# Retention and two MLPs in one kernel: the decay rates come in as one row and are spread over the partitions by a product

## The chip, the cores and the metric

One core of one Trainium2 chip runs the whole program. Five engines with instruction streams of their own take part: TensorE (PE, its weight loads shown apart as PEld), VectorE (DVE), ScalarE (ACT), GpSimd (POOL) and SyncE (SP), which here only issues DMAs. ScalarE and GpSimd issue some DMAs too. The metric is the device time of one execution in microseconds, the median of several runs; lower is better.

## The reference, cut to what matters

```python
q, k, v: (2, 8, 768, 64) float32      lam: (8,) float32, one decay rate for each head
rel   = pos[:, None] - pos[None, :]
Dmask = np.where(rel >= 0, lam[:, None, None] ** rel, 0.0)        # powers of the rate
for each block of 64 positions:
    intra = (q_b @ k_b.T * Dmask) @ v_b
    inter = (q_b * lam ** (pos + 1)) @ state
    out   = intra + inter
    state = lam ** block * state + (k_b * lam ** (block - 1 - pos)).T @ v_b
x = out as (1536, 512)
x = relu(x @ w_in) ** 2 @ w_out            # first MLP, 512 -> 2048 -> 512
y = h @ w_out2,  h = leaky_relu(x @ w_in2) # second MLP, slope 0.01
```

The eight rates enter everything in the first part: the masks, the scaling of queries and keys, and the decay of the state.

## The kernel before, in words

The first part, `retention`, works on 12 units: 2 batches times 6 chunks of 128 positions, all 8 heads together. For each unit the kernel loads k, q and v (256 KB each, `load`), transposes k and q on TensorE (`transposes`, the result copied to `kqT` by ScalarE), makes the scores (`scores`), multiplies them with the table of powers on VectorE (`mask`, result `Pm`), updates the state (`state`, with the scaled keys `kd` made by GpSimd in `scale_k`), and adds up the output (`output`), which is split in a high and a low part (`xhi`, `xlo`) for the MLPs. The MLPs follow; there every matrix product is done in three products of such parts, and some blocks by sums and differences of blocks. Their products all stand in one helper, `three` (L622).

The order on SP and PE within `retention` is the order in which the code is written; on the other engines a scheduler sets it, except where the code pins a step.

At the start, before the first keys are there, the program does three things that the change touches:

- It loads the rates. `rate` is a tile of 128 partitions by 8 heads; one DMA from ScalarE's queue (L229) reads the same 32 bytes for each of the partitions.
- It keeps TensorE busy with products whose result nobody reads, the warming products: `warm(8)` multiplies a tile of zeros, `none`, with itself eight times (L244), and `warm_half(3)` does three small transposes of the identity between the real transposes (L248). Each fp32 product of `warm` shows as two passes in the trace.
- It makes the tables on VectorE: `of_row` from `rate` (L260, two copies), `LR` from `of_row` (L263, four scans) and `powers` from `rate` (L254, eight scans). `mask` and `scale_k` read `powers`; `scale_q` and the decay of the state read `LR`.

TensorE's results stand in a ring of eight banks (`bank`), handed out in the order of the code; a bank comes free when its reader is done. A DMA's completion is counted on one of eight semaphores in turn, so that a later DMA that takes the same semaphore waits until the earlier one has landed.

Of the kernel before, what the change touches and what calls it, by code (L numbers as in the profile page):

```python
# [9 lines left out]
F32 = mybir.dt.float32  # L10
# [6 lines left out]
P = 128  # L17
# [3 lines left out]
def tile_retention_then_two_mlps(  # L21
# [12 lines left out]
    nc = tc.nc  # L34
    B, H, S, D = q.shape
# [22 lines left out]
    def bank():  # L58
        return psum.tile([P, 512], F32, tag="ps", name="ps")
# [150 lines left out]
    def retention(ctx_att, att):  # L210
# [14 lines left out]
            nats[i, name] = t  # L225

        ve = nc.vector
        rate = att.tile([P, H], F32, name="rate")
        nc.scalar.dma_start(rate, bass.AP(tensor=lam.tensor, offset=lam.offset, ap=[[0, P], [1, H]]))  # L229
        for i in range(2):  # L230
            load(i, "k")
            load(i, "q")
# [3 lines left out]
        make_identity(nc, ident)  # L236
        none = att.tile([P, C], F32, name="none")
        ve.memset(none, 0.0)

        idle = bank()  # L240

        def warm(n):
            for _ in range(n):
                tc.keep_in_program_order(nc.tensor.matmul(idle[:, 0:P], none, none, start=True, stop=True))  # L244
# [2 lines left out]
            for _ in range(n):  # L247
                tc.keep_in_program_order(nc.tensor.transpose(idle[:, 0:D], ident[0:D], ident[0:D, 0:D]))  # L248

        warm(8)  # L250

        powers = att.tile([P, H, C + 1], F32, name="powers")
        for h in range(H):
# [182 lines left out]
    with ExitStack() as ctx_att:  # L436
        att = ctx_att.enter_context(tc.tile_pool(name="att", bufs=1))
        with tc.manual_schedule(engines={mybir.EngineType.SP, mybir.EngineType.PE}):
            retention(ctx_att, att)
# [569 lines left out]
```

## Time and profile before

| what | value |
|---|---|
| median of 3 runs | 556.07 us (555.64 to 557.9) |
| the profiled execution, whole time | 556.28 us |
| its span in the trace | 554.5 us |
| PE busy | 548.7 us, 99% of the span |
| DVE, ACT, POOL busy | 78%, 54%, 16% |
| DMA | 71.86 MB, mean 130 GB/s |

The span runs from the first instruction to the last. The whole time is longer than it by 1.78 us, which lie around it. The busy shares are means over the span; how the first 50 us differ from the rest is seen only in the views by stretch.

### The profile page before, as it was taken

What the parts mean: (1) busy time and instruction counts of PE and PEld (TensorE: products, weight loads), DVE (VectorE), ACT (ScalarE), POOL (GpSimd) and SP (SyncE); (2) the same over time, 40 slices, a digit from 0 to 9 for tenths busy, and PEclk for the clock granted to TensorE, in tenths of its full rate; (3) what the DMA queues carried; (4) which work ended last, traced back from release to release, by engine and by line L of the source; (5) the groups of instructions that cost most, each with busy time, mean ns of one, the idle gap of its engine ahead of it and who ended that gap; (6) DMA issues with size and microseconds to landing.
All of it is one profiled execution on the core that took longest, in us unless ns stands there. A gap on an engine that the chain in (4) does not pass through costs nothing.

```text
span 554.5 us, 8716 instructions
## 1 busy us (share of the span) xinstructions
PE 548.7 (99%) x3393; PEld 470.9 (85%) x3393; DVE 434.6 (78%) x643; ACT 299.8 (54%) x482; POOL 87.0 (16%) x99
## 2 busy tenths in 40 slices
PE   8999999999999999999999999999999999999997
PEld 8989888888888888888888889888898889888997
DVE  6669999997775895639999986969176954967987
ACT  4454898556773357453376385645364464546520
POOL 5864000000213011220000000000213011310041
PEclk9999999999999999999999999999999999999999
DMA  9997245542459615674423221264518743650544
GB/s 204 218 259 238 77 160 182 190 149 80 83 150 196 179 19 134 165 139 130 155 57 115 82 100 47 76 229 139 88 21 168 192 102 52 76 78 0 165 141 151
DMA packets 68056, 71.86 MB, mean 130 GB/s; under 512 B 39856, under 2 KB 43952, under 8 KB 68016
## 3 DMA queue, kind: packets, MB, share of 16 engines
q1 hardware_dynamic: 52208, 54.14, 31.2%
q0 software_dynamic: 6912, 12.59, 15.9%
q10 hardware_dynamic: 8896, 4.59, 2.9%
q8 instruction: 26, 0.43, 0.3%
q14 instruction: 14, 0.11, 0.1%
HBM read 49.29 MB, written 22.02 MB: 129 GB/s over the span
## 4 chain that ended last, share of the span: by engine, by line
PE 96%; DMA 3%; SPq 1%; ACT 0%; issue 0%; DVE 0%; ACTq 0%
PE ps L622 90%; PE ps L303 2%; PE ps L365 1%; PE ps L363 1%; DMA v<-in_v 1%; DMA q<-in_q 1%; PE ps L334 1%; DMA k<-in_k 1%; PE ps L282 1%; SPq L65 1%; ACT kqT L286 0%; DVE res L850 0%; ACTq L286 0%
## 5 line engine op out<-in xcount | busy, mean ns | idle before, releaser
L812 POOL DMA_DIRECT2D spill<-f x48 | 42.5, 891 | 401.6 <-ACT f L808 401.6
L808 ACT COPY f<-ps 128x512 f32<-128x512 f32 x72 | 41.9, 585 | 70.9 <-PE ps L622 70.8
L622 PE MATMUL ps<-xlo,w1h 128*128 128x512 f32 (+1 forms) x190 | 69.2, 368 | 0.0
L622 PE MATMUL ps<-xhi,w1l 128*128 128x512 f32 (+1 forms) x184 | 68.3, 371 | 0.0
L622 PE MATMUL ps<-xhi,w1h 128*128 128x512 f32 (+1 forms) x184 | 68.3, 371 | 0.0
L762 DVE TENSOR_TENSOR f<-ps,f 128x512 f32<-128x512 f32 x70 | 46.2, 687 | 6.2 <-PE ps L622 5.8
L622 PE MATMUL ps<-xhi,sw 128*128 128x512 f32 (+1 forms) x176 | 49.6, 350 | 0.0
L172 DVE TENSOR_TENSOR w2l<-hb,w2h 128x1024 fp32r<-128x1024 f32 x16 | 19.6, 1223 | 36.3 <-ACT w2h L170 36.3
L622 PE MATMUL ps<-g0h,w2h 128*128 128x512 f32 x112 | 43.6, 389 | 0.0
L622 PE MATMUL ps<-g0h,w2l 128*128 128x512 f32 x112 | 43.6, 389 | 0.0
L154 DVE SCALAR_TENSOR_TENSOR hb<-raw,hb 128x1024 uint16<-128x1024 uint32 x31 | 42.4, 1366 | 0.3
L622 PE MATMUL ps<-g0l,w2h 128*128 128x512 f32 x112 | 42.6, 389 | 0.0
L622 PEld LDWEIGHTS ps<-xlo,w1h 128*128 128x128 f32 x190 | 35.5, 189 | 6.1
L622 PE MATMUL ps<-t,sw 128*128 128x512 f32 x168 | 40.4, 389 | 0.0
L551 DVE TENSOR_TENSOR g0l<-f,g0h 128x512 fp32r<-128x512 f32 x52 | 35.1, 686 | 6.7 <-ACT f L547 5.9
L145 ACT ACTIVATE hb<-raw 128x1024 f32<-128x1024 f32 x31 | 35.3, 1149 | 9.3 <-DMA raw<-in_moe_w_in 2.9
L622 PEld LDWEIGHTS ps<-xhi,w1l 128*128 128x128 f32 x184 | 34.7, 188 | 6.2 <-DVE w1l L132 0.4
L622 PEld LDWEIGHTS ps<-xhi,w1h 128*128 128x128 f32 x184 | 34.7, 188 | 6.2 <-ACT xhi L70 0.2
L622 PE MATMUL ps<-w2h,g0h 128*128 128x512 f32 (+1 forms) x104 | 39.6, 381 | 0.0
L622 PE MATMUL ps<-w2l,g0h 128*128 128x512 f32 (+1 forms) x104 | 39.6, 381 | 0.0
L622 PE MATMUL ps<-w2h,g0l 128*128 128x512 f32 (+1 forms) x104 | 38.6, 381 | 0.0
L151 DVE SCALAR_TENSOR_TENSOR hb<-raw,hb 128x1024 uint32<-128x1024 uint32 x31 | 37.9, 1221 | 0.3
(220 smaller groups left out, 1321.9 us busy)
## 6 DMA issues: line engine op xcount, KB each, us to landing
raw<-in_moe_w_out SPq DMA_DIRECT2D x15, 1024.0 KB, 4.9
raw<-in_moe_w_in SPq DMA_DIRECT2D x14, 1024.0 KB, 6.6
spill<-f POOLq DMA_DIRECT2D x48, 256.0 KB, 4.3
spill<-f SPq DMA_DIRECT2D x24, 256.0 KB, 2.3
k<-in_k SPq DMA_DIRECT2D x12, 256.0 KB, 5.1
q<-in_q SPq DMA_DIRECT2D x12, 256.0 KB, 5.1
f<-spill SPq DMA_DIRECT2D x12, 256.0 KB, 2.8
res<-spill SPq DMA_DIRECT2D x12, 256.0 KB, 4.8
```

What stands on the lines that cost most here:

```text
L65: step = queue.dma_start(dst, src)
L145: step = nc.scalar.activation(hf, w_hi.bitcast(F32), AF.Abs)
L151: yield ve.scalar_tensor_tensor(out=hb, in0=w_hi, scalar=0xC0000000, in1=hb, op0=ALU.bitwise_and, op1=ALU.bitwise_or)
L154: step = ve.scalar_tensor_tensor(out=half, in0=w_lo, scalar=2.0 ** -29, in1=half, op0=ALU.mult, op1=ALU.add)
L172: yield ve.tensor_tensor(out=lo, in0=hf, in1=hi, op=ALU.subtract)
L282: nc.tensor.transpose(ps[half][:, p] if early else two[half][:, n, p], src[r, 2 * p:2 * p + 2, :].rearrange("s h d -> s (h d)"), ident[r, r])
L303: nc.tensor.matmul(raw_scores[i][par][:, p, :], kT[i][r, p, :], qT[i][r, p, :], start=True, stop=True)
L551: nc.vector.tensor_tensor(out=glo, in0=r, in1=ghi, op=ALU.subtract)
L622: nc.tensor.matmul(ps, a, b, start=start and n == 0, stop=stop and n == len(ops) - 1, skip_group_check=again)
L762: ve.tensor_tensor(out=out, in0=ps[h, where], in1=other, op=ALU.add)
L808: nc.scalar.copy(f, src)
L812: nc.gpsimd.dma_start(dst, f, accum_op=ALU.add)
```

## The change

The DMA now brings the eight rates into a tile of one partition, `row`, as 32 bytes once. A second tile of one partition, `ones`, is filled with 128 ones on VectorE. Where eight warming products stood there are now five, then one product of `ones` (128 columns, one row) with `row` (one row, 8 columns), whose result is the eight rates in each of 128 partitions, and then two more warming products. VectorE copies the result from its bank to `rate`. All that reads `rate` is as before.

```diff
-        rate = att.tile([P, H], F32, name="rate")
-        nc.scalar.dma_start(rate, bass.AP(tensor=lam.tensor, offset=lam.offset, ap=[[0, P], [1, H]]))
+        row = att.tile([1, H], F32, name="row")
+        nc.scalar.dma_start(row, bass.AP(tensor=lam.tensor, offset=lam.offset, ap=[[H, 1], [1, H]]))
...
+        ones = att.tile([1, P], F32, name="ones")
+        ve.memset(ones, 1.0)
...
-        warm(8)
+        warm(5)
+        in_all = bank()[:, 0:H]
+        nc.tensor.matmul(in_all, ones, row, start=True, stop=True)
+        warm(2)
+        rate = att.tile([P, H], F32, name="rate")
+        ve.tensor_copy(rate, in_all)
```

TensorE's instructions at the start of the program, before: a semaphore named `DMAHW` counts a DMA, the others an engine. L244 is a warming product, L282 a transpose of keys or queries, L248 a small warming transpose.

```order
L244 MATMUL ps<-none 128x128 [waits DVE_49]
L244 MATMUL ps<-none 128x128 x7
L282 MATMUL ps<-delta,k 128x64 [waits DMAHW1_49,Pool_49]
L282 MATMUL ps<-delta,k 128x64 x7
L248 MATMUL ps<-delta 128x64 x3
L282 MATMUL ps<-delta,q 128x64 [waits DMAHW2_49]
```

And now, at the same place (the lines after the change are 2 to 7 higher):

```order
L246 MATMUL ps<-none 128x128 [waits DVE_49]
L246 MATMUL ps<-none 128x128 x4
L254 MATMUL ps<-row,ones 128x8 [waits DMAHW0_49,DVE_49]
L246 MATMUL ps<-none 128x128 x2
L289 MATMUL ps<-delta,k 128x64 [waits DMAHW1_49,Pool_49]
L289 MATMUL ps<-delta,k 128x64 x7
L250 MATMUL ps<-delta 128x64 x3
L289 MATMUL ps<-delta,q 128x64 [waits DMAHW2_49]
```

One of the eight large products is gone, another has become the small one, and the wait for the rates' DMA now stands in TensorE's stream, ahead of the first transposes.

VectorE's instructions at the start of the program, before: the wait for the rates' DMA is that of the first copy to `of_row`.

```order
L238 MEMSET none 128x128
L260 COPY of_row<-rate 64x4 [waits DMAHW0_49]
L260 COPY of_row<-rate 64x4
L263 SCALAR_TENSOR_TENSOR LR<-of_row,none 128x128 [waits DVE_49]
L263 SCALAR_TENSOR_TENSOR LR<-of_row,none 128x128 x3
L254 SCALAR_TENSOR_TENSOR powers<-rate,delta 128x129 [waits Pool_49]
```

And now:

```order
L238 MEMSET none 128x128
L240 MEMSET ones 1x128
L257 COPY rate<-ps 128x8 [waits PE_49]
L267 COPY of_row<-rate 64x4 [waits DVE_49]
L267 COPY of_row<-rate 64x4
L270 SCALAR_TENSOR_TENSOR LR<-of_row,none 128x128 [waits DVE_49]
L270 SCALAR_TENSOR_TENSOR LR<-of_row,none 128x128 x3
L261 SCALAR_TENSOR_TENSOR powers<-rate,delta 128x129 [waits Pool_49]
```

The filling of `ones` and the copy to `rate` are new, and the chain of the tables waits for TensorE where it waited for the DMA. On ScalarE the DMA of `rate` has become that of `row` at the same place; on GpSimd and SP, and on all engines behind this start, the order is the same as before. One wait is new there: the first product of `scores` also waits for VectorE, since the bank that it takes is the one from which `rate` was copied.

## Rows read from the trace of the kernel before

**Rows 1.** The page: span, and busy time of the engines.

```profile
span 554.5 us, 8716 instructions
PE 548.7 (99%) x3393; PEld 470.9 (85%) x3393; DVE 434.6 (78%) x643; ACT 299.8 (54%) x482; POOL 87.0 (16%) x99
```

**Rows 2.** Waits of PE, whole span: us in total, times, longest us.

```profile
PE ps L244 <- DVE none L238: 1.1, 1, 1.1
PE ps L334 <- DMA v<-in_v: 0.7, 1, 0.7
PE ps L282 <- DMA k<-in_k: 0.3, 1, 0.3
```

**Rows 3.** Chain of waits, 0 to 60 us: start us, us, what.

```profile
2.87 1.41 SPq L65
4.28 0.04 issue
4.32 4.16 DMA k<-in_k
8.48 0.14 issue
8.62 0.46 PE ps L282 x8
...
29.72 5.32 DMA q<-in_q
35.05 0.02 issue
35.07 5.95 DMA v<-in_v
41.02 0.14 issue
41.15 0.69 PE ps L334 x16
```

**Rows 4.** Busy time by stretch: us, five engines (x instructions), clock, DMA share, GB/s.

```profile
0.00:10.00 10.00, 8.60 (x97) 8.00 (x99) 5.58 (x17) 4.42 (x11) 3.33 (x11) 1.00 0.84 189
10.00:20.00 10.00, 9.93 (x204) 9.01 (x202) 7.34 (x14) 4.09 (x10) 9.69 (x12) 1.00 1.02 230
20.00:30.00 10.00, 9.97 (x202) 9.21 (x199) 6.25 (x12) 3.90 (x7) 6.90 (x8) 1.00 1.01 228
30.00:40.00 10.00, 10.00 (x200) 9.35 (x201) 6.65 (x13) 4.98 (x9) 6.99 (x7) 1.00 1.07 250
```

**Rows 5.** Timeline of PE, from the start: start us, us, instructions.

```profile
1.06 3.79 PE L244 MATMUL ps<-none 128*128 128x128 f32 x16 [1.06 <-DVE none L238]
4.77 0.69 PE L282 MATMUL ps<-delta,k 64*128 64x64 f32 x8
...
6.22 0.46 PE L282 MATMUL ps<-delta,k 64*128 64x64 f32 x8
...
6.94 1.16 PE L303 MATMUL ps<-kqT 64*128 64x128 f32 x16
7.94 0.41 PE L282 MATMUL ps<-delta,q 64*128 64x64 f32 x8
8.62 0.46 PE L282 MATMUL ps<-delta,k 64*128 64x64 f32 x8 [0.27 <-DMA k<-in_k]
9.08 1.16 PE L303 MATMUL ps<-kqT 64*128 64x128 f32 x16
10.07 0.41 PE L282 MATMUL ps<-delta,q 64*128 64x64 f32 x8
10.46 0.69 PE L334 MATMUL ps<-v,kd 128*64 128x64 f32 x16
10.94 1.07 PE L365 MATMUL ps<-Pm,v 128*64 128x128 f32 x16
```

**Rows 6.** Timeline of the DMA of the rates, of DVE and of POOL, from the start.

```profile
0.74 0.45 ACTq L229 DMA_DIRECT2D rate<-in_lam  x1
3.96 0.34 DVE L260 COPY of_row<-rate 64x4 f32<-64x4 f32 x2 [2.96 <-DMA rate<-in_lam]
4.33 1.37 DVE L263 TENSOR_TENSOR_SCAN LR<-of_row,none 128x128 f32<-128x128 f32 x4
5.62 2.62 DVE L254 TENSOR_TENSOR_SCAN powers<-rate,delta 128x129 f32<-128x129 f32 x8
8.16 1.26 DVE L308 TENSOR_TENSOR Pm<-ps,powers 128x512 f32<-128x512 f32 x2
8.33 2.07 POOL L321 TENSOR_TENSOR kd<-k,powers 128x512 f32<-128x512 f32 x2 [6.10 <-DVE powers L254]
```

**Rows 7.** DMA view, 0 to 4 us: queues, and issues with KB and us to landing.

```profile
q1 hardware_dynamic: 1523, 0.39, 42.3%
q10 hardware_dynamic: 144, 0.00, 1.8%
...
rate<-in_lam ACTq DMA_DIRECT2D x1, 4.0 KB, 3.2
```

**Rows 8.** The shortest landing of the program, DMA view, 545 to 555 us.

```profile
out<-res SPq DMA_DIRECT2D x1, 128.0 KB, 1.9
```

**Rows 9.** The first load of k, by its tile, 0.7 to 1 us.

```profile
L65 SPq DMA_DIRECT2D k<-in_k x1: 417/417/417, 0.7 to 0.7; - x1
...
DMA to landing us min/median/max: 3.6/3.6/3.6
```

**Rows 10.** Views of L244 and L248: durations (ns min/median/max), first and last start.

```profile
L244 PE MATMUL ps<-none x16: 421/421/579, 1.1 to 4.4; 128*128 128x128 f32 x16
...
L248 PE MATMUL ps<-delta x9: 223/261/311, 5.3 to 6.6; 64*128 64x64 f32 x9
```

**Rows 11.** Chain of waits, 500 us to the end.

```profile
499.96 50.98 PE ps L622 x383
550.94 0.02 issue
550.97 0.42 DVE res L850
```

## The prediction

> **What bounds the kernel now.** I read the page first. TensorE is busy for 548.7 of 554.5 us [rows 1], so only what moves its stream, or one of its few idle stretches, can move the end. The waits of PE list those: 1.1 us at the start, before the zeros for the first warming product are there, 0.3 us for a load of keys, and 0.7 us for a load of values [rows 2]. Third, the chain of waits says where the last two lie: the keys of unit 2 land at 8.48 us and TensorE goes on at 8.62; the values of unit 8 land at 41.02 and it goes on at 41.15 [rows 3]. No later wait stands in the list, and the chain is products of L622 down to the last addition at 550.97 [rows 2, 11]. So the end is set by the moment at which the stream goes on at 41.15, and this moment by a landing.
>
> Fourth, the stretches [rows 4]. From 10 to 40 us the DMA engines are busy the whole time (1.01 to 1.07) at 228 to 250 GB/s. In the same stretches TensorE is busy for 9.93 to 10.00 of 10 us. The first 40 us are therefore two full streams side by side, loads and products, which meet at 8.62 and at 41.15, and both times TensorE was the one that waited. A change of TensorE's first microseconds that does not move the loads meets a wait of 0.27 us at 8.62 and one of 0.71 us at 41.15, and is lost in them.
>
> **The change part by part.**
>
> *The load of the rates.* Before, it was issued at 0.74 us, took 0.45 us to issue and landed after 3.2 us, at 3.94; the first copy to `of_row` starts at 3.96 [rows 6, 7]. Now it is 32 bytes once. No row shows so small a load. Its landing is bounded by 1.9 us, the shortest of the program [rows 8], and by the 3.2 us of the load that it replaces, which has the same queue, source and moment. That gives 2.64 to 3.94 us for `row`. I take the middle, about 3.2: the old landing counts the last of many packets among those of the first keys, and now there is one to wait for. The Trainium skill (DMA: Bandwidth & Descriptors, Anatomy of one DMA) puts a nearly constant 2.0 us on a transfer, mostly its completion, which it fitted for DMAs that GpSimd issues; by that the row would be there at about 2.75 us, and TensorE would not wait for it at all. No run here shows it yet.
>
> *What the loads gain.* The 144 packets of that queue took 1.8% of 16 engines in 4 us [rows 7], 0.07 us of each engine. If all of that stands in front of the keys, every later landing comes 0.07 us earlier; if it fell in time in which the engines had nothing to do (up to 4 us queue q1 uses 42.3% of them), nothing. I take 0.07, with 0 and 0.1 as ends. That the 0.45 us of issuing on ScalarE shrink is worth nothing: its next work that someone waits for is the copy of transposed keys, behind 4.77.
>
> *TensorE's start.* The 16 passes of the eight products span 3.79 us from 1.06, and a single one is drawn 0.42 long, so one starts every (3.79 - 0.42) / 15 = 0.225 us [rows 5, 10]. Five products are ten passes: the small product could start at 1.06 + 2.25 = 3.3 us. With the row there at 3.2 it does not wait. It too is two passes, of 8 columns where the others have 128; each costs between nothing and 0.225 us, and I take 0.1, nearer to a transpose of 64 columns (eight in 0.69 us with their tail) than to the large ones. Then four passes, 0.9 us. The end of the warming comes at 3.3 + 0.2 + 0.9 = 4.4 us (4.2 to 4.65), against 1.06 + 16 x 0.225 = 4.66 before. The first transposes need the keys of unit 0, which land at 0.74 + 3.6 = 4.34 [rows 9], and before they started 0.11 behind the end of the warming (4.77 against 4.66). They start at about 4.5 now: 0.25 us earlier, with 0 and 0.4 as ends. This gain ends at the keys of unit 2, which landed at 8.48; of it only the 0.07 us of the loads stay.
>
> *VectorE's tables.* The product's result can be read some 0.35 us behind the start of its last pass (the tail of a pass in rows 10 is 0.31): 3.3 + 0.1 + 0.35 = 3.75. The new copy costs about what one to `of_row` costs, 0.17 (two in 0.34) [rows 6], so `of_row` starts at 3.9 to 4.0, against 3.96: no change. The filling of `ones` costs nothing, since VectorE stands idle for 2.96 us there.
>
> What hides a delay of the tables, if the row is late: `Pm` of unit 0 is done at 8.16 + 1.26 = 9.42 and first read at 10.94, and the first `kd` is done at about 8.33 + 1.03 = 9.36 and read at 10.46 [rows 5, 6]. So 1.1 us of delay cost TensorE nothing; without that cover it would cost what exceeds them. The new wait of the first scores, for the bank that `rate` is copied from, ends near 4 us, and they start at 6.94.
>
> **The sum.** Nothing from TensorE's start, nothing from the tables, 0.07 us from the loads, which the stream would feel at 41.15 too. The profiled execution took 556.28 us, 0.21 above the median; 556.28 - 0.07 = 556.21, and against the median 556.07 - 0.07 = 556.0.
>
> **The rivals.**
>
> *The row is late and TensorE waits for it.* At the 3.94 us of the old landing the small product starts at about 3.95, the warming ends at 3.95 + 0.2 + 0.9 = 5.05 and the transposes start near 5.15: 0.4 us late, with 0.6 as the end at full-length passes. The tables come 0.6 to 0.7 late, which their cover of 1.1 takes. Of TensorE's 0.4 to 0.6 the idle 0.27 at 8.62 takes a part and the 0.71 at 41.15 the rest, if the loads stay as they are. If the loads are held back by buffers that TensorE frees later, some of it reaches the end: 0 to 0.5 us, 556.3. For it speaks the queue shared with the keys, against it the single packet.
>
> *Slower: TensorE's clock rises later.* The column of the clock shows 1.00, the level of 2.4 GHz, in all of these stretches [rows 4], but the passes tell that the first ones go slower: eight transposes of keys take 0.69 us at 4.77 and 0.46 at 6.22 [rows 5], and a small warming transpose 311 ns at most and 223 at least [rows 10]. I read this as 1.2 GHz up to about 6.1 us, after five microseconds without a break. Now there is a product of 8 columns among them, and perhaps a pause for the row. If the rise comes as late again, at about 11, the work between 6.2 and 11.2, some 4.7 us, takes 1.5 to 2 times as long: 2.3 to 4.7 us more, less the idle 0.27 at 8.62 and the 0.71 at 41.15, so 1.3 to 3.7, in the middle 558.5. It decides, that is costs over 0.5% (2.8 us), only when the slow level lasts for four to five microseconds more with no wait to hide them. The Trainium skill (TensorE: Matmul & The Clock Gate, Part 1) has the rule that speaks here: the slow clock is the default, and only sustained activity lifts it, at a moment that varies from run to run. The passes of this trace agree with the slow start; whether the small product disturbs the rise, no row shows.
>
> *The whole of retention moves.* If loads wait for buffers more than for the DMA engines, a stream that starts 0.25 to 0.4 us earlier frees buffers earlier, the values of unit 8 come earlier too, and the wait at 41.15 shrinks with them: 0.3 to 0.7 us, 555.5. Against it speaks the DMA share of 1.0 from 10 to 40 us.
>
> **How the numbers follow.** No change at the end (the sum): 0.70, with its own range of 555.7 to 556.7. Late row: 0.12. Later clock: 0.08, half of it above 0.5%. Moved retention: 0.10, which stays under 0.7 us. About 0.5% is what a measurement of this kernel can tell from no change; 1.0 us of waits at 8.62 and 41.15 and a first wait of 1.1 us that the change does not touch are all that could be gained, so faster by more than that has 0.02, left for what I don't see. Slower by more: 0.04. Within: 0.94. The range reaches from the moved retention and its 0.5 us of scatter (single runs lie from 555.64 to 557.9) to the nearer half of the late clock: 555.0 to 557.6.
>
> **What would show it.** In the changed kernel's trace: a landing of `row` in under 2.5 us and no wait of the small product for it; the first transposes at about 4.5; `of_row` at 3.9 to 4.0; TensorE's wait for the keys of unit 2 longer, at about 0.5 us in all, and its transposes at 8.5 to 8.6 as before; the wait for the values at 41 still there, at 0.6 to 0.8 us. It would be wrong if transposes of 64 columns still take 0.69 us for eight behind 6.2 (the clock), if the values of unit 8 land more than 0.5 us from 41.02 (the loads), or if a wait appears behind 41.15, where none was.

## The result and the profile after

The changed kernel takes 560.3 us (560.06 to 560.78, 6 runs) where the kernel before took 556.02 in the same comparison (6 runs): a ratio of 1.0077, 95% interval 1.0066 to 1.0088, slower by 4.3 us. The forecast was 556.0 and no change, with a range up to 557.6. The profiled execution took 560.49 us, its span is 558.7.

Of the page, the span and the engines' busy time, answering to [rows 1]:

```profile
span 558.7 us, 8720 instructions
PE 550.4 (99%) x3393; PEld 471.9 (84%) x3393; DVE 434.7 (78%) x645; ACT 300.2 (54%) x482; POOL 86.8 (16%) x99
```

TensorE runs the same number of instructions (3393) and its busy time is up by 1.7 us only; the span has grown by 4.2. Its waits over the whole span, answering to [rows 2]:

```profile
PE ps L341 <- DMA v<-in_v: 1.2, 3, 0.6
PE ps L246 <- DVE none L238: 1.1, 1, 1.1
PE ps L341 <- POOL tmp L348: 0.8, 1, 0.8
PE ps L310 <- ACT kqT L297: 0.7, 1, 0.7
PE ps L289 <- DMA q<-in_q: 0.5, 2, 0.3
```

Two waits of 1.0 us in all behind the start have become seven of 3.2 us. All of them lie in retention: the timeline of TensorE shows the first product of the MLPs at 56.94 us, where it stood at 52.67 in the kernel before, and the chain's last addition comes at 555.16 instead of 550.97 [rows 11]. So all of the 4.2 us are lost before 57 us. First the line of the kernel before, then two of the changed one:

```profile
52.67 0.50 PE L622 MATMUL ps<-xhi,w1h 128*128 128x512 f32 x1
```
```profile
56.94 0.50 PE L629 MATMUL ps<-xhi,w1h 128*128 128x512 f32 x1
```
```profile
555.16 0.42 DVE res L857
```

The start of TensorE's timeline, answering to [rows 5]:

```profile
1.06 2.50 PE L246 MATMUL ps<-none 128*128 128x128 f32 x10 [1.06 <-DVE none L238]
3.49 0.59 PE L254 MATMUL ps<-row,ones 1*128 1x8 f32 x2
4.01 1.22 PE L246 MATMUL ps<-none 128*128 128x128 f32 x4
5.16 0.69 PE L289 MATMUL ps<-delta,k 64*128 64x64 f32 x8
```

The first transposes come at 5.16 us, 0.39 later than before, where I had expected 0.25 earlier. But 4.3 us cannot come from there alone. The busy time by stretch, answering to [rows 4], in the same columns, says where to look:

```profile
0.00:10.00 10.00, 8.67 (x87) 7.95 (x89) 5.99 (x19) 4.27 (x11) 2.97 (x11) 1.00 1.04 179
10.00:20.00 10.00, 9.27 (x187) 8.24 (x185) 6.55 (x12) 4.01 (x11) 9.01 (x10) 1.00 1.15 212
20.00:30.00 10.00, 8.68 (x177) 8.11 (x174) 5.99 (x13) 3.61 (x7) 6.96 (x8) 1.00 0.97 192
30.00:40.00 10.00, 9.75 (x189) 8.86 (x187) 5.64 (x11) 4.03 (x8) 4.90 (x5) 1.00 1.01 207
```

The last two columns say most. The DMA engines are about as busy as before (0.97 to 1.15 between 10 and 40 us, where it was 1.01 to 1.07) and move less: 212 GB/s instead of 230, 192 instead of 228, 207 instead of 250. The same loads, with the same packets of 256 bytes, go slower. The DMA view of 5 to 15 us, queue q1 alone (packets, MB, share of 16 engines), first of the kernel before, then of the changed one:

```profile
q1 hardware_dynamic: 9297, 2.34, 103.8%
```
```profile
q1 hardware_dynamic: 8597, 2.17, 136.0%
```

The share is the time that the packets took, summed, over the time of 16 engines; the records of packets overlap, which is how it can be over 100%. Of the 160 us that 16 engines have in 10 us, a packet took 1.038 x 160 / 9297 = 17.9 ns before and 1.36 x 160 / 8597 = 25.3 ns now. The landings are later for it. Of the chain, two of its longest pieces, answering to [rows 3]:

```profile
24.78 7.96 DMA q<-in_q
...
39.85 8.81 DMA q<-in_q
```

Nothing in the code of these loads was changed, and their order is the same. What differs is where they land. The tiles of a pool lie one behind another, and the pools too; `row` takes the 32 bytes that `rate` had, `ones` 512 bytes more in each partition and `rate` 32 more. In the built program all buffers of k, q and v therefore stand 544 bytes further on: the first of k at 165120 before, a multiple of 256, and at 165664 now, 32 bytes past one. These two addresses are those of the program as it was built; no view of the traces shows them, and neither the diff nor the order of the instructions does. What they are worth is for the experiments to show.

How the slow packets begin is seen in two short stretches of the changed kernel, 2.5 to 3.5 us and 3.7 to 5 us:

```profile
q1 hardware_dynamic: 1120, 0.28, 125.0%
```
```profile
q1 hardware_dynamic: 1117, 0.28, 129.4%
```

The loads to the moved places run at 283 GB/s at first, with packets of 1.25 x 16 / 1120 = 17.9 ns, and then fall to 217 GB/s with packets of 1.294 x 20.8 / 1117 = 24.1 ns. So a packet to such a place does not have a fixed price; it is a stream of them that is held to a lower rate.

### The profile page after: what moved, and what is told of

Its sections match the earlier page's. It is cut to its first block, busy times and chain, and to the rows that moved or that the text cites. A ratio compares the mean times of both kernels' runs of the same rounds, so it can differ in the third digit from the quotient of the medians.

```text
span 558.7 us, 8720 instructions
## 1 busy us (share of the span) xinstructions
PE 550.4 (99%) x3393; PEld 471.9 (84%) x3393; DVE 434.7 (78%) x645; ACT 300.2 (54%) x482; POOL 86.8 (16%) x99
## 4 chain that ended last, share of the span: by engine, by line
PE 93%; DMA 5%; SPq 1%; POOL 1%; issue 0%; DVE 0%
PE ps L629 89%; DMA q<-in_q 3%; DMA v<-in_v 2%; SPq L65 1%; PE ps L372 1%; PE ps L310 1%; PE ps L370 1%; PE ps L341 1%; PE ps L289 0%; POOL qS L303 0%; POOL tmp L348 0%; POOL kd L328 0%; DVE res L857 0%
```

## The experiments

Four theories stood against each other. A: the loads are slow because they land off a multiple of 256 bytes. B: TensorE's late start and a later rise of its clock. C: the single packet for the rates leaves the DMA engines in another phase. D: the engines' own reading and writing at shifted addresses. Each ratio below is against runs of the kernel before on the same chip, with its 95% interval.

**The shift alone, in the kernel before.**

```diff
         ve.memset(none, 0.0)
+        att.tile([P, 136], F32, name="pad")
```

> The kernel before, its eight warming products and its load of the rates untouched, with an unused tile of 544 bytes in each partition behind the zeros, which moves the buffers of k, q and v from multiples of 256 bytes to 32 bytes past one, as the changed kernel does by its two new tiles. Theory A (the landing addresses slow the loads): as slow as the changed kernel, 559.5 to 560.8 us, 256-byte packets at a mean of 24 to 26 ns between 5 and 15 us instead of 18, first transposes still at 4.77 us. Theory B (TensorE's later start and the later rise of its clock cost the time): 556.0 us, packets at 18 ns. Theory C (one packet for the rates leaves the DMA engines in another phase): 556.0 us, packets at 18 ns.

560.6 us, ratio 1.0092 (1.0077 to 1.0107). An unused tile costs as much as the whole change. The DMA view of 5 to 15 us has the slow packets, 1.332 x 160 / 8611 = 24.7 ns, at 219 GB/s:

```profile
q1 hardware_dynamic: 8611, 2.17, 133.2%
```

A holds; B and C cannot explain this run, since its TensorE program and its load of the rates are those of before. (In its profiled execution the clock also fell back for some 3 us, see the last section; the two kernels shifted by 64 and 128 bytes, slow alike, show a granted clock of 1.00 between 5 and 15 us.) The first transposes came at 4.85 and not at 4.77. The tables and the work tiles moved here too, which the runs below take apart in part.

**The changed kernel, realigned.**

```diff
         ve.memset(none, 0.0)
+        att.tile([P, 56], F32, name="pad")
```

> The changed kernel with 224 unused bytes more, so that all buffers behind the tables move by 768 bytes in all and stand on multiples of 256 bytes again; the small product and the load of one packet are untouched. Theory A: 555.7 to 556.8 us, packets at 18 ns, first transposes still late at 5.16 us and absorbed by the waits at 8.6 and 41 us. Theories B and C: 560.0 to 560.6 us, B with packets that follow from the late start, C with packets at 24 to 26 ns.

556.77 us, ratio 1.0014 (1.0005 to 1.0024). The 224 bytes give 3.5 us back. The packets take 1.176 x 160 / 10519 = 17.9 ns again, at 267 GB/s, and TensorE waits for no load any more, though its first transposes stand at 5.17. B and C fall here a second time; what remains of the loss is 0.8 us. That aligned places have no such lower rate shows in the stretch of 2.5 to 12 us, where this kernel moves 278 GB/s on end, with packets of 1.23 x 152 / 10476 = 17.9 ns:

```profile
q1 hardware_dynamic: 10476, 2.64, 123.0%
```

**The shift by 64 and by 128 bytes.** The kernel before with a pad of `[P, 16]` and of `[P, 32]` at the same place.

> The kernel before with 64 unused bytes: buffers of k, q and v at 64 bytes past a multiple of 256. Theory A says slow if the boundary that counts is 256 bytes (559.5 to 560.8 us), and 556.0 us with packets at 18 ns if it is 64 bytes. I expect 64 (chance 0.6). Theories B and C: 556.0 us either way.

> The kernel before with 128 unused bytes: buffers of k, q and v at 128 bytes past a multiple of 256. Theory A with the boundary at 256 bytes: slow like the shifts by 32 and 64 bytes, 559.3 to 560.8 us against 555.6, packets at 24 to 26 ns between 5 and 15 us. Theory A with a boundary at 128: 555.6 us, packets at 18 ns. I expect 256 (chance 0.8).

64 bytes: 559.86 us, 1.0077 (1.0062 to 1.0092), 220 GB/s between 5 and 15 us. I had thought 64 would be enough, and it is not. 128 bytes: 560.48 us, 1.0078 (1.0056 to 1.0099), 218 GB/s. So 32, 64 and 128 bytes past a multiple of 256 cost the same within their intervals. In both kernels too the first loads run at the full rate, 271 and 278 GB/s between 3.7 and 4.9 us with packets of 18 ns, before the slow packets set in. The changed kernel, whose full stream of loads began about a microsecond earlier, was down at 217 GB/s by then; so the fall follows the stream and not a moment of the program.

**The work tiles alone.** A pool with one tile of 32 bytes between the pools of k, q, v and those of the work tiles.

```diff
+        gap = ctx_att.enter_context(tc.tile_pool(name="gap", bufs=1))
+        gap.tile([P, 8], F32, name="pad")
         tr = ctx_att.enter_context(tc.tile_pool(name="tr", bufs=3))
```

> The kernel before with 32 unused bytes between the buffers of k, q and v, which stay where they were, and the tiles that the engines write and read (kqT, qS, kd, Pm), which move to 32 bytes past a multiple of 64. Theory A: 556.0 us, packets at 18 ns, since no load lands in these. If it is the engines' own reading and writing at such addresses that costs (theory D): 558 to 560.5 us with packets at 18 ns. B and C: 556.0 us.

555.86 us, 1.0009 (0.9999 to 1.002), packets at 1.097 x 160 / 9827 = 17.9 ns. D falls for the work tiles: where the engines write and read these costs nothing that can be told from noise. The tables, which also move with the shift of the whole, were not moved alone.

**The control: 768 bytes in the kernel before**, which puts the buffers where the realigned kernel has them (a pad of `[P, 192]`).

> The kernel before with 768 unused bytes, which puts the buffers of k, q and v at the very places that they have in the realigned changed kernel (multiples of 2048). The eight products and the load of 128 packets are untouched. If the realigned kernel's fuller loads (267 GB/s between 5 and 15 us, against 236 before) come from the places: the same here, 260 to 275 GB/s, no wait for values at 41 us, and 555.0 to 555.6 us. If they come from the rates' single packet: 230 to 240 GB/s here, a wait near 41 us, and 555.5 to 555.9 us.

556.15 us, 1.0005 (0.9992 to 1.0017), 248 GB/s. Another multiple of 256 is as good as the old one. The realigned kernel's 267 GB/s does not come from its places; whether it comes from the single packet stays open, since two other kernels with the single packet had 249 and 246 GB/s in that stretch, and the two aligned ones with 128 packets, this and the one above, 248 and 249.

**Some of the loads.** Gaps of 32 and 224 bytes around one pool: first the values alone at 32 bytes past a multiple of 256 (the diff), then, with the gaps ahead of k and of v, keys and queries alone.

```diff
...
+        for name, n in (("k", 6), ("q", 4), ("v", 4)):
+            if name == "v":
+                gap = ctx_att.enter_context(tc.tile_pool(name="gap", bufs=1))
+                gap.tile([P, 8], F32, name="pad")
...
+        rest.tile([P, 56], F32, name="pad")
```

> The kernel before with the buffers of v alone at 32 bytes past a multiple of 256 (12 of the 36 loads), k and q aligned, work tiles aligned. Theory A: only packets of loads of v are slow; a third of the loads at 24 to 26 ns instead of 18 gives about a third of the loss of 4.3 to 5 us, 556.5 to 557.5 us, or less where their delay is hidden. If not the landing address but something that comes with any shift of the whole is the cause: 555.6 us.

> The kernel before with the buffers of k and q at 32 bytes past a multiple of 256 (24 of the 36 loads) and those of v and the work tiles on multiples of 256. With v alone shifted the loss was 0.4 us, not a third of 4.3 to 5. If the loss is a ceiling on the rate of loads that are all shifted (218 GB/s between 5 and 15 us), which mixing lifts: 556.5 to 558.5 us here and a mean between 220 and 235 GB/s in that stretch. If the loss only needs shifted keys and queries, since TensorE waits for these first: 559.5 us or more.

Values alone (12 of 36 loads): 556.08 us, 1.0007 (0.9998 to 1.0017); no loss that can be told, where I had expected a third. Taken alone this run would also fit a cause other than the landing addresses; the second kernel speaks against that. Keys and queries alone (24 of 36): 558.02 us, 1.0041 (1.0026 to 1.0057), 225 GB/s. The loss is not in proportion. The values' loads lie between aligned ones and the stretch of 5 to 15 us still moves 244 GB/s; where all loads are shifted it moves 218 to 220. That is what a ceiling on the rate of shifted loads looks like: a few of them fit under it, a full stream of them does not. The packets agree: with the values alone shifted they took 1.102 x 160 / 9626 = 18.3 ns in the mean, where a third of them at 25 ns would give about 20. I had put down both outcomes of the second kernel beforehand, and it came out on the ceiling's side. The granted clock fell in its profiled execution too (0.53 between 8 and 11 us, 0.997 over the whole), but its slowest run, 559.42 us, has 1.00, so the clock is not what its loss rests on. The loss of the whole shift is about twice that of keys and queries alone; how the rest divides between the values and the tables stays open.

**The change at the old places.** `row` and `ones` in a pool of their own behind all others.

```diff
+        small = ctx_att.enter_context(tc.tile_pool(name="small", bufs=1))
...
-        row = att.tile([1, H], F32, name="row")
+        row = small.tile([1, H], F32, name="row")
...
-        ones = att.tile([1, P], F32, name="ones")
+        ones = small.tile([1, P], F32, name="ones")
```

> The changed kernel whole, with its two new tiles behind all others, so that the buffers of k, q and v stand exactly where they stood before. What is left is the change itself: TensorE's start late by 0.4 us, the tables late by 0.4 us, one packet for the rates. Theory A: 555.6 to 556.4 us against 555.6 to 555.7, ratio 1.000 to 1.0015, packets at 18 ns, no wait of TensorE for a load before 41 us above 0.3. If the places explain only part of the 4.3 us: 557 us or more.

556.42 us, 1.0004 (0.9995 to 1.0013, 11 runs). With its tiles out of the way the change costs nothing that a measurement can tell. The first transposes still start at 5.17, and TensorE's waits have become these:

```profile
PE ps L247 <- DVE none L239: 1.1, 1, 1.1
PE ps L311 <- ACT kqT L294: 0.5, 1, 0.5
```

The two waits for loads are gone, and one of 0.5 us for the copied queries has come, which fits a late start that was taken by what had been waiting.

**A late start alone: nine products** (`warm(9)` for `warm(8)` in the kernel before).

> The kernel before with nine warming products where it has eight, nothing else: the first transposes start at about 5.2 us, as late as in the changed kernel, with the rates' load and the tables as before. If a late start of TensorE is lost in its later waits, as the prediction has it: 555.6 to 555.9 us, ratio within 0.0008 of 1. If it is carried to the end: 0.4 us, ratio 1.0008. Under theory B as it stood (late start and late clock cost the 4 us): 558 us or more.

556.23 us, 1.0005 (0.9994 to 1.0017). The first transposes start at 5.20, as the line below shows, and 0.43 us of lateness do not show at the end beyond noise; whether a part of the 0.4 us is carried, this interval of 1.3 us cannot say.

```profile
5.20 0.69 PE L282 MATMUL ps<-delta,k 64*128 64x64 f32 x8
```

**The small product earlier.** The realigned kernel with `warm(2)` ahead of the product and `warm(3)` behind it.

> The realigned changed kernel with the small product behind two warming products, and three behind it: five large products where the changed kernel has seven. The row landed at 1.92 us there, so the product does not wait. First transposes at 4.3 to 4.5 us instead of 5.17, since the keys land at 4.3. If TensorE's late start is what is left of the loss (0.8 us, 0.14%, of the realigned kernel), this one takes it back: 555.2 to 556.0 us. If the moment of the clock's rise is what is left: 555.6 to 557 us, scattered as the realigned kernel is, with the clock's rise in the trace the later the slower the run.

556.07 us, 1.0001 (0.9991 to 1.0011). The timeline of TensorE:

```profile
2.21 0.59 PE L255 MATMUL ps<-row,ones 1*128 1x8 f32 x2
2.73 1.65 PE L247 MATMUL ps<-none 128*128 128x128 f32 x6
4.31 0.69 PE L290 MATMUL ps<-delta,k 64*128 64x64 f32 x8
```

The product starts at 2.21 without a wait for the DMA, so the row is there before that, and the transposes start at 4.31, 0.86 earlier than in the realigned kernel. The time is 0.7 us below that kernel's, and lies just outside the range that I had set for a start carried on and inside that for the clock. The single runs of the two kernels lie in 555.13 to 556.8 and 555.59 to 556.89, their intervals overlap, and against the kernel before there is no gain. Where the 0.8 us of the realigned kernel come from stays open.

## Why the prediction was wrong

The step that failed is the one on the loads, "What the loads gain", where I wrote that every later landing comes up to 0.07 us earlier, or at the least not at all. It took the loads' own speed as given and looked only at what stands in the queue. Between 5 and 45 us the loads of k took 6.0 us to land in the median instead of 5.2, those of q 5.9 instead of 5.2 and those of v 5.3 instead of 4.5, since a packet of their queue took 0.943 x 640 / 26923 = 22.4 ns in the mean there and not 0.818 x 640 / 28087 = 18.6 (25.3 and 17.9 between 5 and 15 us). The values of unit 8 landed at 38.3 + 5.4 = 43.7 us instead of 41.02; a landing more than 0.5 us from there was the sign that I had named for the loads. The premise of the argument, that the end follows the loads, was right, and it is why the error was so dear: two full streams side by side had 1.0 us of slack between them, and one of the two lost 8 to 17% of its rate between 10 and 40 us.

It was not among my rivals, and slower by more than 0.5% had a chance of 0.04, though what was needed could be read: the change puts two more tiles into the pool `att`, and the code opens that pool ahead of those of k, q and v. The Trainium skill (DMA: Bandwidth & Descriptors, How a descriptor splits into AXI transactions) says that a transaction has to start at a multiple of 256 bytes, so that a descriptor which starts past one needs one transaction more. By that, as an estimate from the page's rule, 256 bytes at 32, 64 or 128 past a multiple take two where they took one, all three alike. The three equal losses agree with it, and so does the shift by 768. But the page gives the rule for what a transaction reads; here it is the side written, in SBUF, that was shifted, and no run here shows the side read. Nor does a count of transactions say by itself why the first loads to the shifted places ran at 283 GB/s with packets of 17.9 ns. That the landing places of keys and queries cost the time is shown; by what mechanism they hold a stream to 218 to 220 GB/s is not.

Point by point, the rest.

- *The row is there in time*: right, but by more than my bounds allowed. In the changed kernel the two packets of its queue stand in the DMA view of 1.6 to 1.7 us, and in the kernel with the earlier product TensorE used the row at 2.21, ahead of the 2.64 to 3.94 that I worked out from rows. From its issue at 0.74 that is 1.5 us at most, less than the 2.0 us by the Trainium skill (DMA: Bandwidth & Descriptors, Anatomy of one DMA), which would have had it at 2.75.
- *The small product costs 0.2 us*: wrong. The ten passes ahead of it are over at 1.06 + 2.50 - 0.42 + 0.21 = 3.35, the last four started at 4.01 only, and they took 1.22 us with their tail, where four of the steady stream take 0.42 + 3 x 0.21 = 1.05. The transposes came at 5.16 where two passes of 0.1 would have let them start at 4.5. The size of this term was 0.2; it measured 4.01 - 3.35 = 0.66, and with the slower four passes behind it about 0.8. The rival of the late row had named 5.15 for the transposes; that it was met is luck, since the row was not late.
- *The tables do not move*: they moved by 0.36 us, with `of_row` at 4.32 and not at 3.96, inside the cover of 1.1 us that I had worked out. VectorE's rows:

```profile
4.12 0.17 DVE L257 COPY rate<-ps 128x8 f32<-128x8 f32 x1 [2.98 <-PE ps L254]
4.32 0.34 DVE L267 COPY of_row<-rate 64x4 f32<-64x4 f32 x2
```

- *What TensorE's start loses or gains is lost in its later waits*: not contradicted, and not shown. The kernel at the old places and the one with nine products have ratios of at most 1.0013 and 1.0017 at the upper end, and 0.4 us carried to the end would be 1.0008.
- *The rival of the later clock*: the fast passes did come later in the profiled execution, though the column of the clock shows 1.00 there as before. Eight transposes of keys at 6.7 us, one of them apart, still took long (the seven in 0.64 us, where eight took 0.46 before), but the kernel at the old places has this too and is not slower, so it is not what made the 4.3 us.
- *Moved retention, and no rival for loads that slow down*: that rival let the loads move by buffers that come free earlier, and no run shows this. What it had right is that the end moves with the loads. The stretches told that loads and TensorE are balanced; I asked what a gain there is worth and not what could make the loads worse.

## What to carry to other kernels

A new tile moves everything that is laid out behind it. Before a change that adds or resizes a tile in a pool ahead of DMA buffers, look up where these buffers stand before and after, and keep what is loaded in short runs on multiples of 256 bytes, or put small tiles into a pool behind. The sign in the trace is a DMA share that stays or rises while the GB/s fall, at the same packet size; here it cost time where all loads, or two thirds of them, were shifted, and none that could be told where a third was.

## What the runs showed of the hardware that was not expected

Loads in runs of 256 bytes that land 32, 64 or 128 bytes past a multiple of 256 moved 218 to 220 GB/s in a full stretch of 10 us, at 25 ns a packet (23 with 128 bytes), where aligned ones moved 236 to 267 at 18 ns. It is a ceiling on a stream and not a price of each packet: for about the first microsecond at full rate the shifted loads went as fast as aligned ones (283 GB/s between 2.5 and 3.5 us in the changed kernel, at 17.9 ns), and between 16 and 20 us, where the stream of loads has pauses, packets of the changed kernel were back at 0.969 x 64 / 3383 = 18.3 ns.

TensorE's clock can fall back in this start. In the kernel with the unused tile of 544 bytes the transposes run at the fast pace from 4.85 us on (eight in 0.46 us), TensorE then waits 0.48 us for queries and 0.56 us for keys, and the granted clock is at the lower level, 0.50 of 2.4 GHz, from 8 to 11 us:

```profile
4.85 0.46 PE L283 MATMUL ps<-delta,k 64*128 64x64 f32 x8
...
5.96 0.47 PE L283 MATMUL ps<-delta,q 64*128 64x64 f32 x8 [0.48 <-DMA q<-in_q]
...
7.16 0.46 PE L283 MATMUL ps<-delta,k 64*128 64x64 f32 x8 [0.56 <-DMA k<-in_k]
...
7.65 1.79 PE L304 MATMUL ps<-kqT 64*128 64x128 f32 x15
```
```profile
8.00:11.00 3.00, 2.74 (x34) 2.55 (x33) 1.81 (x4) 1.40 (x6) 2.39 (x3) 0.50 1.35 219
```

The kernel with shifted keys and queries shows the same behind waits of 0.43, 0.48 and 0.56 us (0.53 between 8 and 11 us). Such waits did not always bring it: the kernel shifted by 128 bytes waits 0.45, 0.54 and 0.66 us there, and its granted clock stays at 1.00.

The moment from which the passes are fast also differs between executions of almost the same program. The scores of unit 0 start at 7.46 us both in the realigned kernel and in the one at the old places; fifteen passes took 2.02 us in the first (556.83 us in all) and 1.24 in the second (555.96):

```profile
7.46 2.02 PE L311 MATMUL ps<-kqT 64*128 64x128 f32 x15
```
```profile
7.46 1.24 PE L311 MATMUL ps<-kqT 64*128 64x128 f32 x15
```

This may be a part of the scatter of 2 us that all aligned kernels show (555.08 to 557.41 in the runs of one comparison); it was not followed up.
